# Requesting two half-blocks of input earlier and moving their on-chip transposes, in a fused convolution and feed-forward kernel

## The chip, the cores and the metric

The kernel runs on one core of a Trainium2 chip. The metric is device microseconds of one execution. "Draw" stands below for what differs by chance between two executions of one kernel. The span that the profile shows (first to last instruction) is about 1.7 us shorter than the time of the same execution.

Engines are named as in the profile: PE (TensorE, matmuls and transposes), DVE (VectorE), ACT (ScalarE), POOL (gpsimd, which here mostly issues DMAs), SP (which issues the other DMAs).

## The reference

Two stages. The first is a depthwise causal convolution of 7 taps with softmax weights per head; the second is a feed-forward layer without biases, with a leaky ReLU.

```python
w = softmax(weight)                                     # 8 heads x 7 taps
x = conv(x_pad, w)                                      # 8 x 4096 x 192
h = x @ w_in                                            # 192 -> 2048
g = np.maximum(0.01 * h, h)
out = g @ w_out                                         # 2048 -> 192
```

## The kernel before

x is needed with its channels on the partitions. Two batch rows are worked on at once, in blocks of 512 positions. The first five blocks are halved ("half-blocks" of 256), which is meant to fill the pipeline sooner. For most blocks a DMA on POOL's queue casts x to bf16 (`load_x`) and a DMA on SP's queue transposes it (`transpose_x`). The first two blocks go another way: their four halves, 0 to 3, are loaded in fp32 (`load_first`), cast on DVE or ACT (`cast_first`), transposed on PE (`transpose_first`) and copied out of PSUM (`evac_first`). The change is about halves 2 and 3.

The convolution of a half-block is done one half-block ahead, on DVE: three channel groups, each with one `tensor_scalar` (line L175 of the profile) and six `scalar_tensor_tensor` (L181). Only some channel groups of halves 0 and 1 are convolved on PE instead (L200). PE then runs, for each unit `u` of a half-block, twelve matmuls into a buffer `ph` (of which there are two) and ACT empties it with the activation. The second product follows in slots between the units.

```python
    def load_first(q, after=None):
        t = stage_pool.tile([128, 2, HS, D], FP32, name="x_nat")
        for e in range(2):
            ins = nc.sync.dma_start(out=t[:, e, :, :], in_=...)
            if after is not None and e == 0:
                tc.add_manual_dep(ins.ins, after.ins.name, ...,
                    reason="leave the DMA engines to the weights")
    ...
    for i, grp in enumerate(groups):
        ...
        for j in range(steps):
            for u in range(2 * j, 2 * j + 2):
                act = mm1(grp, u)
                ...
                if i == 0 and u in (0, 6):
                    load_first(2 + u // 6, act)
                if i == 1 and u in (2, 3):
                    cast_first(3, u - 2, nc.scalar.copy)
            for _ in range(quota):
                mm2_slot(slot)
                slot += 1
            if i == 0 and j == 3:
                evac_y(nc.vector.tensor_scalar_mul)
                for e in range(2):
                    cast_first(2, e, nc.vector.tensor_copy)
                transpose_first(2)
                evac_first(2, nc.vector.tensor_copy, nc.vector.tensor_copy)
            if i == 1 and j == 1:
                nc.gpsimd.tensor_copy(out=pjunk, in_=g[0][0:1, NFC - 1, 1, HT - 1 : HT])
                load_x(2)
            ...
            for job in ahead[per * j : per * (j + 1)]:     # the next half-block's convolution on DVE
                job()
            if i == 1 and j == 1:
                transpose_first(3)
                evac_first(3, nc.vector.tensor_copy, nc.vector.tensor_copy)
```

## Time and profile before

| | kernel before |
|---|---|
| time, median of the first 3 runs | 698.53 us (698.39 to 698.67) |
| span of the profiled run (its time 699.26 us, so longer than those three) | 697.6 us |
| PE, DVE, ACT busy | 99%, 78%, 73% |
| date of the first activation (ACT) | 14.02 us |
| date of half 2's copies out of PSUM (DVE) | 22.81 us |
| PE resumes at the first full block, after its wait for DVE | 119.90 us |

The three dates are the ones to keep. Everything that the change touches lies before the last of them, and what follows it is the same PE work in every version: from there to the end of the span it is 577.6 to 577.7 us in all 19 profiles (of 20) in which PE waits at this place. In the list of instructions in order of time, a line gives the start in us, the time to the end of the group in us, engine, line of the program, operation, what it wrote and read, and in brackets the idle time before it with what ended it.

### The profile page before, as it was taken

The page shows a single profiled execution, that of the slowest core. Times are in us where ns is not written, and L with a number is a line of the kernel's source. Part 1 is how long each engine was busy: PE and PEld are TensorE (multiplying, and loading weights), DVE is VectorE, ACT ScalarE, POOL GpSimd, SP SyncE. Part 2 cuts the span into 40 slices and gives each one's busy share as a digit, 9 for nine tenths or more (in the row PEclk, how much of TensorE's full clock was granted, in tenths as well). Part 3 has the DMA queues.
Part 4 walks back from the last instruction along what each step waited for, and adds up shares of the span by engine and source line. Part 5 has one row for each costly group of instructions (what it writes and reads, how often), then busy time and mean ns, then how long its engine had stood idle before and what let it go on. Part 6 is the DMA issues. An engine that isn't in the chain of part 4 may idle for free.

```text
span 697.6 us, 26016 instructions
## 1 busy us (share of the span) xinstructions
PE 689.2 (99%) x11762; PEld 608.4 (87%) x11762; DVE 543.1 (78%) x1005; ACT 512.2 (73%) x576; POOL 139.6 (20%) x195
## 2 busy tenths in 40 slices
PE   8999999999999999999999999999999999999997
PEld 6799998678888888888888888888888888888887
DVE  6899999967777787777787777787777787777712
ACT  6788887977777777777777777777777777777770
POOL 3632221410222210222211222210222211000000
PEclk9999999999999999999999999999999999999999
DMA  9988553845566545556635556634566626122112
GB/s 171 108 97 96 83 77 77 85 72 81 73 71 92 81 69 81 70 72 90 84 65 82 68 77 85 87 69 75 76 75 82 91 63 77 55 52 58 47 36 70
DMA packets 184015, 54.39 MB, mean 78 GB/s; under 512 B 148320, under 2 KB 183136, under 8 KB 183904
## 3 DMA queue, kind: packets, MB, share of 16 engines
q0 software_dynamic: 97936, 14.17, 29.1%
q1 hardware_dynamic: 85968, 38.56, 22.6%
q8 instruction: 92, 1.51, 0.9%
q14 instruction: 19, 0.16, 0.1%
HBM read 29.88 MB, written 25.17 MB: 79 GB/s over the span
## 4 chain that ended last, share of the span: by engine, by line
PE 86%; DVE 11%; DMA 2%; ACT 1%; issue 1%; SPq 0%; ACTq 0%
PE po L388 43%; PE ph L367 41%; DVE yt L181 9%; DMA x_nat<-in_x_dram 1%; ACT g L374 1%; DVE yt L175 1%; PE acc L200 1%; PE warm L249 1%; DMA xt<-x_bf 1%; PE ptr L142 0%; DVE x_bf L127 0%; ACT x_bf L127 0%; DVE diag L296 0%; ACT yt L329 0%; SPq L430 0%
## 5 line engine op out<-in xcount | busy, mean ns | idle before, releaser
L374 ACT ACTIVATE g<-ph 128x1024 bf16<-128x1024 f32 x512 | 496.3, 1021 | 163.0 <-PE ph L367 163.0
L181 DVE SCALAR_TENSOR_TENSOR yt<-xt,wk,yt 128x512 bf16<-128x512 bf16 (+1 forms) x648 | 442.5, 683 | 17.6
L388 PE MATMUL po<-w_out,g 64*128 64x192 bf16 (+1 forms) x8048 | 397.9, 243 | 0.0
L388 PEld LDWEIGHTS <-g 64*128 64x128 bf16 (+1 forms) x8048 | 371.9, 94 | 29.0 <-issue 0.2
L367 PE MATMUL ph<-yt,w_in 64*128 64x512 bf16 (+1 forms) x3552 | 391.7, 347 | 2.1 <-ACT g L374 0.9
L367 PEld LDWEIGHTS <-w_in 64*128 64x128 bf16 x3552 | 247.4, 94 | 48.9 <-issue 5.6
L78 POOL DMA_DIRECT2D x_bf<-in_x_dram x180 | 133.6, 773 | 420.7 <-DMA xt<-x_bf 418.2
L427 DVE COPY o_sb<-po 128x192 f32<-128x192 f32 x216 | 77.3, 358 | 127.2 <-PE po L388 124.9
L175 DVE TENSOR_SCALAR yt<-xt,wk 128x512 bf16<-128x512 bf16 (+1 forms) x108 | 36.4, 337 | 0.3 <-DMA xt<-x_bf 0.3
L427 ACT COPY o_sb<-po 128x192 f32<-128x192 f32 x40 | 13.0, 325 | 0.0
L249 PE MATMUL warm<-zero 128*128 128x256 bf16 x24 | 5.8, 404 | 1.1 <-DVE junk L217 1.1
L200 PE MATMUL acc<-xt,diag 64*64 64x256 bf16 x84 | 6.6, 318 | 0.0
L200 PEld LDWEIGHTS <-diag 64*64 64x64 bf16 x84 | 5.2, 126 | 1.3 <-DVE xt L156 0.4
L249 PEld LDWEIGHTS <-zero 128*128 128x128 bf16 x24 | 2.8, 134 | 2.5 <-DVE junk L217 1.1
L304 ACT ACTIVATE diag<-ident,whm 128x64 bf16<-128x64 bf16 x14 | 3.6, 336 | 1.9 <-DVE whm L290 1.9
L156 DVE COPY xt<-ptr 128x384 bf16<-128x384 bf16 x7 | 2.2, 353 | 1.9 <-PE ptr L142 1.8
L474 POOL COPY pjunk<-g 1x1 bf16<-1x1 bf16 x1 | 0.2, 177 | 16.5 <-ACT g L374 16.5
L142 PEld LDWEIGHTS <-x_bf 64*128 64x128 bf16 x48 | 1.1, 101 | 2.7 <-ACT x_bf L127 1.9
L142 PE MATMUL ptr<-ident,x_bf 64*128 64x64 bf16 x48 | 1.6, 202 | 1.5 <-ACT x_bf L127 0.9
L127 DVE CAST x_bf<-x_nat 128x384 bf16<-128x384 f32 x5 | 2.3, 453 | 0.7 <-DMA x_nat<-in_x_dram 0.7
L329 ACT ACTIVATE yt<-acc,rsum 128x256 bf16<-128x256 f32 x2 | 0.9, 474 | 2.5 <-PE acc L200 2.5
L237 POOL DMA_DIRECT2D w_in<-in_moe_w_in_dram x4 | 2.6, 659 | 0.0
(34 smaller groups left out, 13.1 us busy)
## 6 DMA issues: line engine op xcount, KB each, us to landing
out_dram<-o_sb SPq DMA_DIRECT2D x128, 192.0 KB, 2.1
x_bf<-in_x_dram POOLq DMA_DIRECT2D x180, 64.0 KB, 3.1
x_nat<-in_x_dram SPq DMA_DIRECT2D x8, 192.0 KB, 4.3
w_in<-in_moe_w_in_dram POOLq DMA_DIRECT2D x4, 384.0 KB, 9.5
xt<-x_bf SPq DMA_TRANSPOSE x90, 2.4
w_out<-in_moe_w_out_dram POOLq DMA_DIRECT2D x1, 768.0 KB, 16.2
w<-in_weight_dram SPq DMA_DIRECT2D x1, 0.2 KB
```

What stands on the lines that cost most here:

```text
L78: nc.gpsimd.dma_start(out=t[:, c, :, e, :], in_=src[2 * rp + e, :, :, c * CH : (c + 1) * CH],)
L142: nc.tensor.transpose(out=ts[i][:, s, c, :], in_=x_bf[q // 2][ps, c, (q % 2) * HS + s, :, :].rearrange("p e k -> p (e k)"), identity=ident ...
L175: lambda s=src, d=dst, c=c: nc.vector.tensor_scalar_mul(d, s, wk[:, c, 0:1])
L181: lambda s=src, d=dst, c=c, k=k: nc.vector.scalar_tensor_tensor(out=d, in0=s, scalar=wk[:, c, k : k + 1], in1=d, op0=mybir.AluOpType.mult, ...
L200: lambda k=k, p=p, a=a, e=e, ps=ps: nc.tensor.matmul(out=acc[ps, :T], lhsT=diag[c][ps, p, k, :], rhs=xt[0][ps, c, a : a + T], start=(k == ...
L237: nc.gpsimd.dma_start(out=w_in[e * CH : (e + 1) * CH, :, fs], in_=moe_w_in[:, fs].rearrange("(c p) f -> p c f", p=CH),)
L249: nc.tensor.matmul(out=wa[:, 0, 0:HT], lhsT=zero[:, 0:128], rhs=zero, start=True, stop=True)
L304: nc.scalar.activation(out=diag[c][:, 1, k, :], in_=ident2, func=mybir.ActivationFunctionType.Copy, scale=whm[:, c, 1, k : k + 1],)
L367: nc.tensor.matmul(out=ph[:, e, i * T : (i + 1) * T], lhsT=w_in[ps, c, f * 128 : (f + 1) * 128], rhs=y[ps, c, t0 : t0 + T], start=(c == 0) ...
L374: act = nc.scalar.activation(out=g[blk][:, nf * u : nf * (u + 1), :, t0 : t0 + T], in_=ph.rearrange("p e (i t) -> p i e t", i=nf), func=my ...
L388: ins = nc.tensor.matmul(out=po[m], lhsT=g[b][ps, fc, e, s * 128 : (s + 1) * 128], rhs=w_out[ps, fc, :], start=(rt != 1 and fc == 0), stop ...
L427: copy(out=o_sb[:, n % 2, :], in_=po.pop(n))
```

## The change

Half 2's x is requested when the first conv copy is done (before the first activation), and half 3's x earlier too. Half 2's transposes move from the end of half 0 to behind the first unit of half 1. Half 3's casts and transposes move from the middle of half 1 to its end. The intent is to take three waits out of the first 30 us: DVE's for half 2's x, PE's for its cast, and PE's for half 3's casts on ACT. The numbers of warm-up matmuls in the start are shifted a little.

```diff
-    warm(9)
+    warm(10)
...
-    warm(3)
+    warm(4)
     select(wps_l, 2)
-    warm(5)
+    warm(4)
...
+    cast_first(0, 1, nc.scalar.copy)
     diag_low(0, range(2))
-    cast_first(0, 1, nc.scalar.copy)
     transpose_first(0)
-    warm(5)
+    warm(4)
...
-        evac_y(act_scale)
+        act = evac_y(act_scale)
         if c == 0:
             warm(2)
+            load_first(2, act)
...
-                if i == 0 and u in (0, 6):
-                    load_first(2 + u // 6, act)
-                if i == 1 and u in (2, 3):
-                    cast_first(3, u - 2, nc.scalar.copy)
+                if i == 0 and u == 3:
+                    load_first(3, act)
+                if i == 1 and u == 0:
+                    transpose_first(2)
+                    evac_first(2, nc.vector.tensor_copy, nc.vector.tensor_copy)
+                if i == 1 and u in (4, 5):
+                    cast_first(3, u - 4, nc.scalar.copy)
...
-                transpose_first(2)
-                evac_first(2, nc.vector.tensor_copy, nc.vector.tensor_copy)
...
-            if i == 1 and j == 1:
+            if i == 1 and j == 3:
                 transpose_first(3)
```

More of the change, by code (lines that the diff above doesn't have):

```diff
@@ L328, in act_scale @@
     def act_scale(out, in_, scale):
-        nc.scalar.activation(
+        return nc.scalar.activation(
             out=out, in_=in_, func=mybir.ActivationFunctionType.Copy, scale=scale
```

## The prediction

> **What bounds the kernel now.** I read the page's chain of waits first, to learn which engines carry the end of the run.
>
> ```profile
> PE 86%; DVE 11%; DMA 2%; ACT 1%; issue 1%; SPq 0%; ACTq 0%
> ```
>
> TensorE (PE) carries most of it, but VectorE (DVE) has 11%, about 77 us, and the change touches only the first 45 us of 697.6. So the question is where those DVE pieces lie. The chain in order of time has DVE's convolution (L175, L181) without a break from 44.59 us to 119.86 us, and PE almost alone after 124 us. I therefore asked for the waits from 30 us to the end, and for PE's and DVE's instructions around 119 us.
>
> ```profile
> PE ph L367 <- DVE yt L181: 0.8, 1, 0.8
> DVE yt L175 <- DMA xt<-x_bf: 0.3, 1, 0.3
> ```
>
> After 30 us PE waits for another engine exactly once: 0.8 us for DVE. The timeline of PE puts that wait at the first full block, after ten half-blocks:
>
> ```profile
> 118.51 0.63 PE L367 MATMUL ph<-yt,w_in 64*128 64x512 bf16 x4
> 119.90 1.04 PE L367 MATMUL ph<-yt,w_in 64*128 64x512 bf16 x8 [0.76 <-DVE yt L181]
> ```
>
> So the first 120 us are a race of two engines. PE arrives at 119.14 and DVE delivers the last channel group at 119.86. What follows is PE at its own pace (about 578 us) and does not change. The end moves only if DVE's date of 119.9 moves: time gained on PE alone becomes a longer wait at this place. In numbers, if DVE comes D earlier and PE comes P earlier, the gain is the smaller of D and P + 0.76.
>
> DVE's own gaps before that date decide D. Its timeline, from the start of half 1 on:
>
> ```profile
> 17.31 3.09 DVE L181 SCALAR_TENSOR_TENSOR yt<-xt,wk,yt 128x256 bf16<-128x256 bf16 x6
> 20.32 0.48 DVE L206 TENSOR_SCALAR yt<-acc,rsum 128x256 bf16<-128x256 f32 x1
> 20.80 0.42 DVE L127 CAST x_bf<-x_nat 128x384 bf16<-128x384 f32 x1
> 21.94 0.43 DVE L127 CAST x_bf<-x_nat 128x384 bf16<-128x384 f32 x1 [0.72 <-DMA x_nat<-in_x_dram]
> 22.81 0.62 DVE L156 COPY xt<-ptr 128x384 bf16<-128x384 bf16 x2 [0.44 <-PE ptr L142]
> 23.46 0.29 DVE L175 TENSOR_SCALAR yt<-xt,wk 128x256 bf16<-128x256 bf16 x1
> ...
> 44.59 0.29 DVE L175 TENSOR_SCALAR yt<-xt,wk 128x256 bf16<-128x256 bf16 x1 [0.28 <-DMA xt<-x_bf]
> ```
>
> The reader is to see three gaps after 20 us: 0.72 us for half 2's x, 0.44 us for its transposes on PE, and 0.28 us at 44.3 for block 2's transposed x. Together 1.44 us, the most that a rearrangement of halves 2 and 3 can give DVE.
>
> [...] of two equal sets of convolution matmuls the first took 3.19 us and the second 1.72 us.
>
> ```profile
> 7.51 3.19 PE L200 MATMUL acc<-xt,diag 64*64 64x256 bf16 x28
> 10.64 0.40 PE L249 MATMUL warm<-zero 128*128 128x256 bf16 x2
> 10.97 1.72 PE L200 MATMUL acc<-xt,diag 64*64 64x256 bf16 x28
> ```
>
> [...] The trace has 6.43 us for the second piece of half 2's x, issued at 15.48 while w_out was still arriving (issued at 5.50, landed 16.2 us later).
>
> **The change part by part.**
>
> 1. *Half 2's x requested at about 11.3 us in place of 15.07* (the first ScalarE (ACT) conv copy ends at 11.22). With the 6.4 to 7.3 us that such a piece took, it lands at about 18 to 18.7, before DVE comes to the cast at 20.8. The 0.72 us wait goes; the casts end at about 21.65. The bytes (2 x 192 KB, some 2 us at the 190 GB/s of this stretch) push the tail of w_in, which landed at about 16.3, toward 17.8; its second half is first used at 18.43. Half 3's x at 17.95 instead of 22.3 pushes w_out from 21.7 toward 23; its first use is at 23.9. Both close, neither binding by this estimate.
>
> 2. *Transposes of half 2 move behind the first unit of half 1.* PE's unit needs a free `ph` buffer, and there are two, so it waits for ACT.
>
> ```profile
> 19.30 3.88 ACT L374 ACTIVATE g<-ph 128x1024 bf16<-128x1024 f32 x4 [1.40 <-PE ph L367]
> 23.47 1.94 ACT L374 ACTIVATE g<-ph 128x1024 bf16<-128x1024 f32 x2 [0.29 <-PE ph L367]
> ```
>
> The four activations start 0.95 us apart ((3.88 - 1.02) / 3). The third ends at 19.30 + 2 x 0.95 + 1.02, about 22.25, and frees the buffer. So the unit runs from about 22.30 for 0.66 us (24 matmuls in 1.31 us, half of them) to 22.96. The twelve transposes follow; before, DVE's copy came 0.39 us after the first of them (22.42 to 22.81). So the copy starts at about 23.35, which is **0.54 us later** than 22.81, although the x is there 2 us early: DVE waits 1.7 us in a row (21.65 to 23.35) where it had waited 1.16 in two pieces. PE and ACT gain: ACT loses its 0.29 us gap.
>
> 3. *Half 3's casts and transposes leave the middle of half 1.* Before, ACT's two casts (0.41 us each on its path) and the transposes behind them held PE for 0.87 us at 28.03 to 28.90. By the ACT pace, half 1's third step starts at about 26.9 against 29.25, and after the transposes' 0.35 us at its end PE reaches half 2 at about 32.5 instead of 34.35. But half 2's convolution on DVE is then not done. It starts at 23.35 + 0.65 = 24.0, has 21 operations worth 10.06 us (23.46 to 34.06, less 0.54 for half 3's copies that lay between), and ends at 34.07. So PE waits about 1.5 us there, a wait that takes the place of those removed. P comes out near 0.4.
>
> 4. *Half 3's copies* (0.54 us) now follow that convolution. The same work in another order: half 3's convolution ends at 44.31 + 0.54 = 44.85.
>
> 5. *Block 2's transposes* are requested behind an output store that waits for ACT, so they come P = 0.4 earlier, landing near 44.2. That is no longer the limit, and the 0.28 us gap disappears. Block 2's convolution begins at about 44.85 instead of 44.59: DVE is **0.26 us later**.
>
> 6. *The start.* Ten instead of nine and four instead of three warm matmuls lie before the second weight selection, at 0.235 us each: 0.4 us or so. DVE's copy of the selected weights (4.39) came right behind that selection, so the first transposes slip by as much. One warm matmul is then saved before the convolution, so it starts at about 7.85 instead of 7.58. [...] The early ACT cast gives nothing, since the transposes also wait for DVE's cast, which moves with the weights.
>
> Sum: +0.54 - 0.28 + 0.1, about +0.4 us on DVE's date, and none of P counts. That is 698.9.
>
> **The rivals.** [...] the first conv set takes 1.7 us in place of 3.2, and half 0 starts about 1.1 us earlier, as soon as w_in allows. The old kernel would have lost such a lead in its wait for x; the new one passes it to DVE: +0.4 - 1.1, or about 697.8. [...] *PE bound, DVE no limit.* Were the first 30 us only PE's, the 1.9 us of point 3 would all be won: 696.6. For it speaks PE's 86% of the chain; against it the measured wait at 119.1. *Weights late.* x ahead of w_in or w_out stalls PE at 13.2, 18.4 or 23.9; each stall adds up to 1 us: 699.5. *Hidden anyway:* the x wait of 0.72 us is real but replaced: 698.5.
>
> **Range and chances.** I weigh the sum (698.9) most, the lucky window (697.8) next, and late weights (699.5) less, which centres on 698.6. [...] Two per cent would be 14 us, ten times the sum of all gaps that the change can touch, so "within 2%" is all but certain.
>
> **What would show it.** In the changed kernel's trace: no DVE wait for half 2's x, but one wait of about 1.7 us for the transposes; the copy at about 23.3; no ACT casts before 26 us; PE reaching half 2 near 32.5 and waiting over 1 us for DVE; no wait at block 2's first convolution; PE's wait at the first full block longer than 0.76 us or about equal. I would be wrong [...] if the casts still waited for x, or if PE stood for weights.

The sum is +0.54 - 0.28 + 0.1, about +0.4 us, or 698.9 us. Its term +0.1 (the start): no trace showed that term, so it stands as the author's estimate; without it the sum is +0.26, about 698.7. The author's estimate is the "up to 1 us" for a stall on late weights. The rival of 697.8 starts from the two sets of before (3.19 and 1.72 us); its -1.1 us is an estimate, and "lucky window" is its name for a first conv set of about 1.7 us. The traces show this: DVE stood idle for 0.44 us ahead of half 2's copies in before (22.81) and for 1.89 us in the changed kernel (23.30), and started half 2's convolution behind them (23.46 and 23.96).

## The result, and the profile after

The changed kernel took **699.95 us** (median of 4 runs, 699.65 to 700.03); before, on the same chip, took 698.46 us (median of 4). The ratio is 1.0021, 95% interval 1.0003 to 1.0038. A ratio here is the mean time of one kernel's fast runs over that of the other's fast runs of the same rounds, so it is not quite the ratio of the medians. The class is "same" (within 2%), but the time lies above every time that the prediction works out (the highest is 699.5), and the change loses time.

DVE in order of time in the changed kernel, without the L181 lines; these answer to DVE's lines in the prediction:

```profile
20.67 0.74 DVE L127 CAST x_bf<-x_nat 128x384 bf16<-128x384 f32 x2
23.30 0.62 DVE L156 COPY xt<-ptr 128x384 bf16<-128x384 bf16 x2 [1.89 <-PE ptr L142]
23.96 0.29 DVE L175 TENSOR_SCALAR yt<-xt,wk 128x256 bf16<-128x256 bf16 x1
27.29 0.55 DVE L175 TENSOR_SCALAR yt<-xt,wk 128x256 bf16<-128x256 bf16 x1
30.88 0.66 DVE L175 TENSOR_SCALAR yt<-xt,wk 128x256 bf16<-128x256 bf16 x1
34.58 0.61 DVE L156 COPY xt<-ptr 128x384 bf16<-128x384 bf16 x2
35.23 0.29 DVE L175 TENSOR_SCALAR yt<-xt,wk 128x256 bf16<-128x256 bf16 x1
38.56 0.55 DVE L175 TENSOR_SCALAR yt<-xt,wk 128x256 bf16<-128x256 bf16 x1
...
45.47 0.28 DVE L175 TENSOR_SCALAR yt<-xt,wk 128x256 bf16<-128x256 bf16 x1
```

The wait for x is gone: both casts run back to back. In its place stands one wait of 1.89 us for PE's transposes, and half 2's copies start at 23.30 instead of 22.81. Three of the `tensor_scalar` operations take 0.55, 0.66 and 0.55 us; the others take 0.28 or 0.29. (In before two of the same six were stretched, to 0.35 and 0.48.) Block 2's first operation (45.47) no longer waits for its transposes, but it starts 0.88 us later than before (44.59).

PE in the changed kernel (its lines L368 and L389 are L367 and L388 of before):

```profile
22.28 0.83 PE L368 MATMUL ph<-yt,w_in 64*128 64x256 bf16 x12 [0.20 <-ACT g L375]
22.93 0.35 PE L142 MATMUL ptr<-ident,x_bf 64*128 64x64 bf16 x12
...
33.72 0.33 PE L142 MATMUL ptr<-ident,x_bf 64*128 64x64 bf16 x11 [0.29 <-ACT o_sb L428]
33.88 0.39 PE L368 MATMUL ph<-yt,w_in 64*128 64x256 bf16 x4
34.72 1.27 PE L368 MATMUL ph<-yt,w_in 64*128 64x256 bf16 x20 [0.44 <-DVE yt L181]
...
45.61 1.27 PE L368 MATMUL ph<-yt,w_in 64*128 64x256 bf16 x20 [0.20 <-DVE yt L181]
...
120.66 1.04 PE L368 MATMUL ph<-yt,w_in 64*128 64x512 bf16 x8 [0.99 <-DVE yt L181]
```

The first two lines are the reason for DVE's wait: the unit has to wait for ACT to free a buffer (0.20 us), and the transposes stand behind it. The last line is the end of the race: PE resumes at 120.66 instead of 119.90, and it waited 0.99 us for DVE instead of 0.76. So the profile of after is 0.76 us behind that of before, and all of it is DVE's lateness. PE itself came to this place at 119.67, later than before (119.14), as it had stood for DVE on the way, for 0.44 us at half 2 and for 0.20 us at half 3. The spans differ by 0.7 us (698.3 against 697.6).

The medians of the timed runs differ by twice that. Part of this is the draw. The profiled execution of before was a long one (699.26 us), and over all jobs the kernel before ran 58 times with a mean of 698.75 us (697.33 to 700.08, standard deviation 0.57) and the changed kernel 19 times with a mean of 699.65 (698.08 to 700.34, 0.61). The difference of means is 0.90 us, with a standard error of about 0.16 (from the two deviations and counts). That is the effect to explain; the 1.49 of the first job is on its high side. (The ratios of the four jobs in which the changed kernel ran are 1.0021, 1.0010, 1.0007 and 1.0013; the intervals of the second and third contain 1.)

### The profile page after: what moved, and what is told of

It is laid out like the page before. It is cut to its first block, busy times and chain, and to the rows that moved or that the text cites. A ratio compares the mean times of both kernels' runs of the same rounds, so it can differ in the third digit from the quotient of the medians.

```text
span 698.3 us, 26015 instructions
## 1 busy us (share of the span) xinstructions
PE 689.9 (99%) x11762; PEld 611.4 (88%) x11762; DVE 543.0 (78%) x1005; ACT 512.3 (73%) x576; POOL 139.6 (20%) x195
## 3 DMA queue, kind: packets, MB, share of 16 engines
q1 hardware_dynamic: 85968, 38.56, 22.9%
## 4 chain that ended last, share of the span: by engine, by line
PE 84%; DVE 13%; ACT 1%; issue 1%; ACTq 0%
PE po L389 42%; PE ph L368 41%; DVE yt L181 12%; DVE yt L175 1%; PE acc L200 1%; ACT g L375 1%; PE warm L249 1%; DVE xt L156 0%; PE ptr L142 0%; DVE diag L296 0%; DVE o_sb L428 0%; PE wps L279 0%; DVE x_bf L127 0%; DVE whm L290 0%; DVE zero L215 0%
## 5 line engine op out<-in xcount | busy, mean ns | idle before, releaser
L181 DVE SCALAR_TENSOR_TENSOR yt<-xt,wk,yt 128x512 bf16<-128x512 bf16 (+1 forms) x648 | 442.5, 683 | 17.6
L389 PE MATMUL po<-w_out,g 64*128 64x192 bf16 (+1 forms) x8048 | 398.6, 243 | 0.0
L389 PEld LDWEIGHTS <-g 64*128 64x128 bf16 (+1 forms) x8048 | 372.6, 94 | 28.8 <-ACT g L375 0.2
L368 PE MATMUL ph<-yt,w_in 64*128 64x512 bf16 (+1 forms) x3552 | 393.0, 347 | 3.0 <-DVE yt L181 1.6
L368 PEld LDWEIGHTS <-w_in 64*128 64x128 bf16 x3552 | 250.4, 94 | 48.1 <-issue 7.0
L127 ACT CAST x_bf<-x_nat 128x384 bf16<-128x384 f32 x3 | 1.5, 509 | 1.6 <-DMA x_nat<-in_x_dram 1.6
```

The source lines that it names most:

```text
L181: lambda s=src, d=dst, c=c, k=k: nc.vector.scalar_tensor_tensor(out=d, in0=s, scalar=wk[:, c, k : k + 1], in1=d, op0=mybir.AluOpType.mult, ...
L368: nc.tensor.matmul(out=ph[:, e, i * T : (i + 1) * T], lhsT=w_in[ps, c, f * 128 : (f + 1) * 128], rhs=y[ps, c, t0 : t0 + T], start=(c == 0) ...
L389: ins = nc.tensor.matmul(out=po[m], lhsT=g[b][ps, fc, e, s * 128 : (s + 1) * 128], rhs=w_out[ps, fc, :], start=(rt != 1 and fc == 0), stop ...
```

## The experiments

Two readings help throughout: the date of half 2's copies counted from the first activation, and the date at which PE resumes at the first full block counted from those copies. The first shows what the order of requests and transposes does; the second shows the rest of DVE's stretch. Starting at the first activation removes what differs from draw to draw.

| order of half 2 | profiles | copies minus first activation, us |
|---|---|---|
| x late, transposes at the end of half 0 | before, r1, r2, b2, d5 | 8.79, 8.70, 8.71, 8.92, 8.80 |
| x early, transposes behind half 1's first unit | after, a1 to a4, p1, q1, q3, d4 | 9.32 in all nine |
| x early, transposes at the end of half 0 | r3, r4, d1, r3 again | 8.30, 8.29, 8.29, 8.29 |
| x early, transposes one unit earlier still | d2, q2 | 7.38, 7.96 |

### How much does one kernel vary? (r1, a1)

Both kernels were run again without any edit.

> The kernel before, unchanged, to learn how its executions differ. The profile on record (span 697.6 us) is some 0.8 us longer than its timed runs imply (698.46 us less the 1.7 us that lie between span and time in the changed kernel). Theory: in most executions half 2's x lands before VectorE asks for it, so the 0.72 us wait of the recorded profile is absent, and the span is near 696.8. Rival: the wait is always there and the difference is elsewhere.

> The changed kernel, unchanged, as the first job showed that executions of before differ by over 2 us[...]. Theory[...]: this one also spreads, from about 698 to 700. Rival (the change itself costs 1.5 us): 699.6 to 700.0 again in all.

Before took 697.33 to 699.70 us in five runs (median 698.07), after 698.52 to 700.34 (median 699.28, ratio to before 1.0010, interval 0.9998 to 1.0023). The expectation for r1 missed: its profiled run had the wait for x again (0.80 us), and it was one of the two long runs of the five (699.61 us). Short executions of before were not caught in a profile, so what they look like stays open. The profile of a1 shows one source of the spread. (In the first jobs the first conv set took 3.19 and 3.12 us in before and r1, and 1.72 in r2, r3 and r4.) PE's first conv set and DVE's copies of half 1, first in the changed kernel's recorded profile, then in a1, the same kernel:

```profile
7.55 3.13 PE L200 MATMUL acc<-xt,diag 64*64 64x256 bf16 x28
12.97 0.62 DVE L156 COPY xt<-ptr 128x384 bf16<-128x384 bf16 x2 [1.34 <-PE ptr L142]
```

```profile
7.43 1.72 PE L200 MATMUL acc<-xt,diag 64*64 64x256 bf16 x28 [0.39 <-DVE xt L156]
11.54 0.61 DVE L156 COPY xt<-ptr 128x384 bf16<-128x384 bf16 x2
```

The same 28 matmuls took 3.13 us in one execution and 1.72 in the other. The granted clock does not tell the two apart: it reads 1.00 over the slower set, and its mean over a1's profiled execution is 1.0. Why the set is faster in one execution is not shown. "Early set" below means a first conv set of 1.72 us; where the set was not listed whole (d1, d2, q1, q2), it is known by half 1's copies at 11.54 or 11.55 us, as in a1. "Late set" means those copies at 12.85 to 13.10 us (p1, with 2.63 us and 12.46, lies between). The whole chain shifted with it: the first activation 13.98 and 12.45, half 2's copies 23.30 and 21.77, the span 698.3 and 696.7. So one profile of each kernel is not enough for differences of under 1 us, and dates have to be counted from the first activation.

### Taking the first set's draw away (a2, b2)

More warm-up matmuls fill PE's gap ahead of the first transposes, in the changed kernel and in the kernel before.

```diff
     select(wps_l, 2)
-    warm(4)        # the changed kernel; warm(5) in the kernel before
+    warm(7)
```

> The changed kernel with three more warm-up matmuls behind the second weight selection, so that TensorE has no gap from 1.1 us to its first transposes[...]. Theory: the first conv set takes about 1.7 us in the profile, the spread shrinks, and the median lies 0.5 to 1 us below the changed kernel's, no more since w_in then is waited for. Rival[...]: no difference.

> The kernel before with two more warm-up matmuls in the same place. With the kernel a2 beside it, the two differ by the change alone[...]. Theory: VectorE's wait for half 2's x takes up most of the lead (copies at 22.3 to 22.8), so it is 0 to 0.5 us faster than before. If the change as such costs, it is faster than the gap-filled changed kernel by 0.3 to 1 us.

Both profiles have the early set (1.72 us). The gain expected for a2 did not come, as PE then stood for the weights (1.22 us in a2); this is PE's line at the first unit in b2:

```profile
12.76 1.48 PE L367 MATMUL ph<-yt,w_in 64*128 64x256 bf16 x23 [1.24 <-DMA w_in<-in_moe_w_in_dram]
```

a2 took 699.59 us (median; 699.31 to 701.49, ratio to before 1.0020, interval 1.0006 to 1.0033), b2 698.57 (698.38 to 699.22, ratio 1.0000, 0.9987 to 1.0012). Side by side on one chip, the change costs 1.0 us of median. So its cost is not the first set's draw, provided that the runs without a profile had the early set too, which is not shown. The spread that a2 was to shrink did not shrink.

### The parts one by one (r2, r3, r4, d4, d5)

r2 is the kernel before with the start's edits alone (the first three pieces of the diff).

> Only the start's edits (warm-up matmuls moved, the scalar cast ahead of the diagonal scales). Theory: nothing, within 0.2 us of before[...]. Rival: the start costs part of the 1.5 us, then 0.4 us or more slower.

Ratio 1.0000 (0.9988 to 1.0013): no effect of the start's edits is seen; the interval leaves room for 0.8 us either way.

r3 is the kernel before with the early requests alone.

```diff
+            load_first(2, act)          # behind the first conv copy
...
-                if i == 0 and u in (0, 6):
-                    load_first(2 + u // 6, act)
+                if i == 0 and u == 3:
+                    load_first(3, act)
```

> Only the early requests of half 2's and half 3's x; transposes and casts where they were. Theory: VectorE's casts run at 20.7 without a wait, PE transposes at about 22.0, the copies start at about 22.35 instead of 22.81; 0 to 0.5 us faster than before. Rival: x ahead of the weights costs, PE waits for w_in or w_out and the run is slower by 0.5 us or more.

> The kernel before with only the early requests, again. Theory: half 2's copies 8.3 us after the first activation in place of 8.8, so 0.2 to 0.6 us faster than before in the mean. Rival: no different from before.

In both profiles half 2's copies come 8.3 us after the first activation, half a microsecond sooner than in before. The first job gave 697.64 us (ratio 0.9991, 0.9978 to 1.0003), the second 698.61 (0.9997, 0.9985 to 1.0009). The mean of the eleven runs is 698.47, 0.3 below that of before; no interval excludes equality. A cost of early x is not seen.

r4 is the changed kernel with half 2's transposes and copies back at the end of half 0.

```diff
-                if i == 1 and u == 0:
-                    transpose_first(2)
-                    evac_first(2, nc.vector.tensor_copy, nc.vector.tensor_copy)
...
                     cast_first(2, e, nc.vector.tensor_copy)
+                transpose_first(2)
+                evac_first(2, nc.vector.tensor_copy, nc.vector.tensor_copy)
```

> The changed kernel with half 2's transposes and copies put back behind its casts, at the end of half 0. Theory: the copies start at about 22.35 instead of 23.30, VectorE is some 0.9 us earlier all the way to the first full block, and about 0.9 of the 1.5 us comes back. Rival (VectorE's stretched tensor-scalar operations beside the gpsimd DMA issues are the main loss): less than half of it comes back.

The copies came at 8.29 us after the first activation, as expected, 1.03 sooner than in the changed kernel. Yet the time was 699.43 us, ratio 1.0009 (0.9997 to 1.0022), close to the changed kernel's ratios: less came back than the 0.9 us expected. DVE's line in r4 says where it went:

```profile
33.59 0.62 DVE L156 COPY xt<-ptr 128x384 bf16<-128x384 bf16 x2 [0.90 <-PE ptr L142]
```

DVE is now early for half 3's copies, and these stand 0.90 us for the transposes that the change put at the end of half 1. In the changed kernel DVE was too late to notice.

d4 is the changed kernel with half 3's casts (`u in (2, 3)`) and transposes (`j == 1`) back in the middle of half 1; d5 is the kernel before with only these moved to the end.

```diff
-                if i == 1 and u in (4, 5):         # d4; in d5 the other way round
-                    cast_first(3, u - 4, nc.scalar.copy)
+                if i == 1 and u in (2, 3):
+                    cast_first(3, u - 2, nc.scalar.copy)
...
-            if i == 1 and j == 3:
+            if i == 1 and j == 1:
                 transpose_first(3)
```

> The changed kernel with half 3's casts and transposes back in the middle of half 1. Theory (half 2's place and the bad phase against gpsimd cost, half 3's move is neutral since VectorE is late anyway): within 0.4 us of the changed kernel, 699.3 to 699.9. Rival (half 3's move costs): 0.5 us or more faster than the changed kernel.

> The kernel before with only half 3's casts and transposes moved to the end of half 1. Theory: TensorE's 0.87 us wait at 28 us goes, but VectorE has half 2's convolution still to finish and sets the end; within 0.4 us of before, and VectorE waits for half 3's transposes for under 0.5 us. Rival (as in r4, where VectorE stood 0.90 us for them): 0.5 us or more slower than before.

d4 took 699.46 us (ratio 1.0015, 1.0003 to 1.0027), like the changed kernel, as the theory had it. Its profile is better than that: from the same first activation (13.98) PE resumes at the first full block at 120.11, 0.55 us before the changed kernel (120.66); the times do not show it. d5 took 699.13 (1.0012, 1.0000 to 1.0024), slower than expected; its profile shows only 0.22 us of wait for half 3's transposes, so the reason of this 0.8 us is not shown. The three together suggest that the two moves do not add. Each makes DVE stand for PE, once for half 2 (9.32 us in d4) and once for half 3 (0.90 us in r4), and undoing one leaves the other to be met. But the intervals of r4, d4, d5 and the changed kernel overlap, so how the cost divides between the moves is not shown. Both undone, with early x kept and without the start's edits, is r3, and that is the only one of them whose mean is not above that of before: 698.47 us against 699.65 of the changed kernel.

### The stretched operations (p1, q1, q3, a3, a4)

In five profiles of the changed kernel (after, a3, a4 with the late set, a1 and, with the filled gap, a2 with the early one) the same three operations take 0.54 or 0.55, 0.66, and 0.55 to 0.57 us. POOL's DMA issues run beside them, in the changed kernel:

```profile
23.32 8.90 POOL L78 DMA_DIRECT2D x_bf<-in_x_dram  x12
34.61 4.45 POOL L78 DMA_DIRECT2D x_bf<-in_x_dram  x6 [2.39 <-ACT o_sb L428]
```

Twelve issues in 8.90 us are 0.742 each. The sixth ends at 23.32 + 6 x 0.742 = 27.77, the stretched operation of 27.29 at 27.84; the eleventh at 31.48, that of 30.88 at 31.54. So the operation ends 0.06 or 0.07 us after an issue. What links the two is not shown. POOL starts when half 0's last activation is done (its `pjunk` copy, at 23.21, is released by ACT), and in the changed kernel DVE's copies hang on the activations too: they start 0.02 or 0.03 us apart in all five profiles (23.30 and 23.32 here). The phase of the two engines is thereby the same every time. In the orders with late x it varies: the stretch over half 2's and half 3's convolutions (the six operations' time less six times 0.28 us) was 0.28 us in before, 0.37 in r1 and in r2, 0.48 in d5, and 1.03 in b2, against 0.94 or 0.95 in the changed kernel.

p1 removes the copy `pjunk`, which holds POOL back, so that the issues come earlier.

```diff
-                nc.gpsimd.tensor_copy(out=pjunk, in_=g[0][0:1, NFC - 1, 1, HT - 1 : HT])
                 load_x(2)
```

> The changed kernel without the gpsimd copy that holds back the block loads, so that gpsimd issues them from about 7 us and is done with the first twelve by about 17 us. Theory (a tensor-scalar operation of VectorE is stretched while gpsimd writes a DMA): in half 2's convolution (between half 2's and half 3's copies) all three tensor-scalar operations take 0.28 to 0.29 us, and the convolution 10.0 us instead of 10.6. Rival: they are stretched all the same. The weights land later, so the run's time says nothing.

DVE's operations of half 2's convolution in p1:

```profile
23.78 0.28 DVE L175 TENSOR_SCALAR yt<-xt,wk 128x256 bf16<-128x256 bf16 x1
27.11 0.28 DVE L175 TENSOR_SCALAR yt<-xt,wk 128x256 bf16<-128x256 bf16 x1
30.43 0.28 DVE L175 TENSOR_SCALAR yt<-xt,wk 128x256 bf16<-128x256 bf16 x1
```

All three are short, and half 2's convolution with the way to the next copies takes 10.13 us (23.78 to 33.91) instead of 10.62. POOL was not quite as early as expected: it waited for DMAs in flight (longest for w_out, 4.47 us) and issued five of the loads between 22.9 and 27.3. So p1 shows that the stretch depends on the phase against POOL. Does it cost time at the end? q1 keeps the change and lets POOL issue only behind each `tensor_scalar`, in batches; q3 does so for half 2's convolution alone.

```diff
-                load_x(2)
+                load_x(2, {4: k0[1, 1]})      # the fifth issue waits for channel group 1's tensor_scalar
+                load_x(3, {1: k0[1, 2]})      # q3; q1 gates three more batches, into half 3's convolution
```

> The changed kernel with the block loads' issues held so that gpsimd issues two to four at a time, each batch released by the tensor-scalar operation that opens a channel group, so none is being written when the next such operation starts. Theory (the stretch is a cause of the loss): all six tensor-scalar operations of half 2's and half 3's convolutions take 0.28 to 0.30 us in the profile instead of 0.92 us over, the two convolutions together 20.0 to 20.2 us, and the runs are 0.4 to 0.9 us faster than the changed kernel's on the same chip. Rival (the stretch is absorbed later): the operations are short, the time is the same.

> The changed kernel again, for comparison on this chip. Theory: stretches of 0.27, 0.38 and 0.27 us on the same three operations as in the two profiles before, and half 2's copies 9.32 us after the first activation; median 699.3 to 700.

> The changed kernel with only the twelve issues beside half 2's convolution gated (four, three, five), block 4's left free. Theory: the two stretched operations of half 2's convolution are short (0.65 us less), a third in half 3's convolution may stay, block 2's transposes are not waited for; the first full block starts 0.3 to 0.7 us earlier for the same date of half 2's copies (after: 97.36 us from copies to that date), and the median is 0.3 to 0.7 us below the changed kernel's. Rival: a wait for block 2's transposes appears again, or the time is unchanged.

> The changed kernel for comparison on this chip: the same three stretches, 97.3 us from half 2's copies to the first full block, median 699.3 to 700.

In q1 all six operations took 0.28 or 0.29 us, but the time was 699.81 us (median) beside 699.70 of a3. DVE now had a new wait, for block 2's transposes: from the first request (39.28) to the end of DVE's wait (45.36) it was 6.1 us, beside loads that POOL now issued between 38.2 and 43.4, where in the changed kernel's recorded profile the three took 2.4 to 3.8 us to land:

```profile
45.36 0.29 DVE L185 TENSOR_SCALAR yt<-xt,wk 128x256 bf16<-128x256 bf16 x1 [1.32 <-DMA xt<-x_bf]
```

In q3 the three operations of half 2's convolution were short and no such wait arose. From copies to the first full block q3 needs 97.08 us, and a4 97.41. The runs' means are 699.57 and 699.82, the ratios to before 1.0009 (0.9997 to 1.0021) and 1.0013 (1.0001 to 1.0025). So the two stretched operations are shown as a cost of 0.65 us on DVE (0.27 + 0.38); that this costs the end about 0.3 us is what these two profiles say and what the times can't separate from noise. The expected 0.3 to 0.7 us of median did not come (0.10).

### A faster version? (d1, d2, q2)

d1 is r3 with the gap filled. d2 also puts half 2's casts, transposes and copies between the seventh and the eighth unit of half 0. q2 is d2 with the gated issues of q1.

```diff
+                if i == 0 and u == 6:
+                    evac_y(nc.vector.tensor_scalar_mul)
+                    for e in range(2):
+                        cast_first(2, e, nc.vector.tensor_copy)
+                    transpose_first(2)
+                    evac_first(2, nc.vector.tensor_copy, nc.vector.tensor_copy)
```

> The kernel before with the early requests (r3) and the filled warm-up gap (b2) together; half 2's transposes and half 3's casts where they were. From the traces so far: half 2's copies come 8.4 us after the first activation when they follow the last unit of half 0 directly (r3, r4), 9.3 to 9.5 us when they stand behind the first unit of half 1 (changed kernel, a1, a2, p1), and at a fixed 22.5 to 22.8 where the late x holds them (before, r1, r2, b2). Theory: copies at about 21.9 and 0.4 to 1 us faster than before. Rival (early x delays w_in by as much): no gain.

> d1 with half 2's casts, transposes and copies one unit earlier, between the seventh and the eighth unit of half 0, where TensorE waits for a free buffer anyway. Theory: copies at about 20.9, VectorE about 1 us ahead of d1 there, but half 3's transposes then wait for its casts; 0.8 to 1.5 us faster than before. Rival: the wait moves to half 3's copies in full and d2 equals d1.

> d2 (early x, filled warm-up gap, half 2's transposes between two units of half 0) with gpsimd's issues gated as in q1. Theory: VectorE is no limit at the first full block (in d2 it was none already), so little is gained over d2 (median 698.83) beyond the draws of w_in's landing; faster than the changed kernel by 0.8 to 1.5 us and about equal to or up to 0.8 us faster than before.

d1 took 698.68 us and d2 698.83 beside 698.36 of before (ratios 1.0002 and 1.0007, both intervals with 1 in them): no gain. d1's expected 0.4 to 1 us and d2's 0.8 to 1.5 us did not come. In d2 DVE is ahead at last (copies 7.38 us after the first activation), and PE passes the first full block without a wait:

```profile
118.36 1.70 PE L368 MATMUL ph<-yt,w_in 64*128 64x512 bf16 x12
```

That is as far as DVE's side goes. What remains is PE's own path, in that profile with 1.53 us of wait for w_in. q2 came to 699.68 (ratio 1.0010, 0.9998 to 1.0023); there w_in was not waited for, but DVE waited 2.00 us for half 3's transposes and 1.94 us for block 2's, as in q1, and PE stood 1.27 us for DVE at the first full block. So d2's passage without a wait may owe something to its late w_in. No version was shown to beat the kernel before.

## Why the prediction was right or wrong

**The race of two engines** held: DVE sets the date at the first full block. But PE gained nothing. After 30 us it waits for DVE three times (1.6 us together, 0.99 of it at the first full block) and once for ACT (0.29), and it came there 0.53 us later than before, where the prediction had it 0.4 earlier.

**Parts 1 and 2** held, the copies to a few hundredths: casts at 20.67 without a wait, no wait for the weights, copies at 23.30 (23.35 predicted) after a wait of 1.89 us (1.7). The table shows the step in general: 9.32 us from the first activation in nine profiles against a mean of 8.78 in before, r1, r2 and b2, which is +0.54.

**Part 3** was wrong on PE's pace. It took half 1's steps at ACT's pace, so that the third begins at about 26.9. It began at 27.78, 2.62 us after the second (25.16), and PE shows no wait between 22.28 and 33.20: the pace was PE's own work. PE came to half 3's transposes at 33.2, not at about 32.1, and waited 0.29 us for ACT and 0.44 us for DVE instead of 1.5. This does not touch the end, which DVE sets.

**Part 4 is the term that failed.** It took DVE's work after half 2's copies for a fixed length. "10.06 us" for half 2's convolution was read from one profile in which the three `tensor_scalar` operations took 0.29, 0.35 and 0.28 us. After the change they took 0.29, 0.55 and 0.66, and the convolution 10.62 us (23.96 to 34.58). With half 3's, the six operations took 2.62 us instead of 1.96, +0.66, where the prediction had "the same work in another order". Half 3's copies, now between the two convolutions, took 0.65 us (34.58 to 35.23), not 0.54. The prediction does not say what POOL does at those dates.

**Part 5** came true by luck: the 0.28 us wait for block 2's transposes vanished, but they were not requested 0.4 us earlier; they were requested 0.14 us later (40.65 against 40.51). DVE came to them at 45.47, where it had come at 44.31. **Part 6** held in size, with -0.04 us at the first activation instead of +0.1; but the conv set began at 7.55, not at about 7.85.

The sum, on the two recorded profiles: copies +0.49 (which has the start in it), operations +0.66, block 2's wait -0.28, and -0.11 left for later pieces of DVE's chain, in all +0.76 instead of about +0.4. From the copies on that is +0.27 where the prediction had -0.28. Over all profiles the picture is flatter: from copies to the first full block, before, r1, r2 and b2 need 97.22 us in the mean, the changed kernel 97.33 (after, a1 to a4). There the gain of part 5 is used up and no more: 0.54 + 0.11 = 0.65, against 0.90 +- 0.3 by the times. The rest is within the noise and stays open. The stretch is not peculiar to the change either. Over the 24 `tensor_scalar` operations of a half-block between the copies and the first full block, the time above 0.28 us each, with the wait for block 2's transposes, comes to 0.99, 1.41, 0.98 and 1.37 us in before, r1, r2 and b2, and to 1.14 to 1.29 in the changed kernel: means of 1.19 and 1.21. The recorded profile of before, from which the prediction read its lengths, was a lucky one.

**The lucky window was no reason to go lower.** The sum's 698.9 was pulled to 698.6 by the rival of a first conv set of 1.7 us, on the argument that "the old kernel would have lost such a lead in its wait for x; the new one passes it to DVE". The draws exist (a1: 696.7 us of span), but the argument was wrong where it was tried: in r2 and b2, with the early set, the old order's copies come 8.71 and 8.92 us after the first activation, as with the late set (8.79 and 8.70): the request hangs on that activation, and the x wait did not take up the lead. (The lead there was only 0.2 to 0.4 us, as PE stood for w_in; a lead of 1.5 us in the old order was not caught in a profile.) A draw that helps both kernels alike is no reason to lower one.

## What to carry to other kernels

When two engines race to the same date, price a reordering on the engine that arrives last, instruction by instruction behind each wait; filling the other engine's gaps can only make it wait longer (in d5 PE's 0.87 us wait went, and its wait at the first full block was 1.20 us instead of 0.76). A request moved earlier is worth nothing if the instruction behind it is moved behind something later: here the x was on time and DVE stood 1.89 us for its transposes. And before reading a term from a single profile at the level of 0.1%, look at what the shared engines do at that date, and at a second execution.

## What stays open

- Why a `tensor_scalar` is stretched beside some POOL issues and not beside others. Operations that began 0.10 us into a DMA issue (before, 23.46 in the issue from 23.36) and 0.64 us into one, 0.10 us before its end (after, 23.96 in the issue from 23.32), took 0.29 us, unstretched, while those that began 0.26 and 0.14 us into one (after, 27.29 and 30.88) took 0.55 and 0.66 us and ended 0.07 and 0.06 us past its end.
- What becomes of the first conv set's draw at the end of a kernel. Here the first activation moved by 1.5 us (12.45 and 13.98) and the span by 1.6 us, of a kernel whose single runs spread over 2.3 us.
- How far the landing of a DMA spreads between executions. w_in made PE wait at the first unit between 0 (a1) and 1.53 us (d2) among executions with the early set, which are of several variants.
- How much DMAs that run together delay each other. Block 2's DMA transposes were waited for until 6.1 us after the first request in q1, beside casting loads; in the changed kernel's recorded profile they landed after 2.4 to 3.8 us.
